# Attention and two feed-forward layers on one core: the places of three kinds of DMA in SyncE's queue, and the pools of three kinds of buffers

## The chip, the cores and the metric

The kernel runs on one core of one Trainium2 chip. The metric is the device time of one execution in microseconds; the median of several runs is taken. Lower is better.

## The reference, cut to what matters

```python
# 4 batches, 12 heads, 448 tokens, 64 per head; all float32
q_n, k_n = rmsnorm(q, g_q), rmsnorm(k, g_k)
scores = 1 / sqrt(64) * q_n @ k_n.T                 # per batch and head
attn = exp(scores - max(scores))
attn = attn / (sum(attn) + 1e-09)
x = (attn @ v)                                      # gathered to 1792 tokens x 768
h = x @ w_in;  x = (h * sigmoid(h)) @ w_out         # layer 1: 768 -> 2048 -> 768
h = x @ w_in2; out = relu(h) ** 2 @ w_out2          # layer 2: 768 -> 2048 -> 768
```

## The kernel before, in words

**Stages.** Attention comes first, over 24 pairs of heads (4 batches of 6 pairs). Layer 1 follows in eight segments, then layer 2 in two halves. Products of float32 are made of three products each: every operand is split into an upper and a lower part (`x_hi`/`x_lo`, `w_hi`/`w_lo`, helpers at L515, L517, L524).

**One pair in attention.** `prepare` loads queries and keys into one `qk` buffer (`load_qk`, L538; four such buffers), squares them on ScalarE (L549), sums (L558), takes the inverse root by Newton steps on GpSimd (L588 to L603), multiplies (`norm`, L612) and turns the result with TensorE (L624). `values` loads the values (`load_v`, L656). `weigh` makes the scores of 112 queries at a time (L677), their maxima (L688), the exponentials and their sums (L695), and turns the exponentials (L704). `attend` works on the sums: it inverts them on VectorE (L724, L725), stores them to DRAM (`store_r`, L732, buffer `rd`), and reads them back spread over 64 partitions for each of the two heads (`spread`, two DMAs at L741, buffer `R`, two of them). Meanwhile TensorE makes the products with the values in two blocks of 16 matmuls (L753), ScalarE copies them to `xf` (L503), and GpSimd multiplies by `R` (`attended`, L776). For the first two batches (12 pairs) the result is split at once into the operands of layer 1 (`x_hi` on ScalarE, L515; `x_lo` on GpSimd, L524). For the other 12 pairs it is stored to DRAM (`keep_x`, L808) and loaded again in layer 1 (`load_x`, L821).

**The order of the work.** A planner (class `Plan`) simulates the engines and writes out one order for each. Every step of attention has a nominal time: `PERIOD` (10.424) times the number of the pair, plus an entry of `LOADS` or `TABLE`, plus an entry of `FIRST` for the first four pairs. On each engine these fixed steps go out in the order of nominal times; the times themselves are not waited for. Steps without a nominal time (all weights, layer 1, layer 2) are put where the simulation finds them ready, and in front of a fixed step only if they end before that could begin. The simulation holds a DMA to land at its own time, plus `extra` for `store_r`. All DMAs are issued by SyncE, in one queue, and an instruction that waits there holds up all behind it.

**Weights.** A unit of weights is loaded in raw form into one of two `raw` buffers (`load_raw`, L869), made into words by one ScalarE instruction (L876) and four of VectorE (L880 to L896), written to DRAM (L904), and split (L515/L517, L524). The first two units are loaded at the start; the third needs the first `raw` buffer back, which its last reader (L896) frees.

**Pools.** Buffers made by `sa` lie in the pool `ap` of the attention stage, those by `sb` in `cp`, which lasts the whole run, or, if asked, in `yp`. `yp` takes the place of `ap`: the step `swap_pools` waits for every step that touches a buffer of `ap`, and each first use of a buffer of `yp` waits for that step. The hidden activations of layer 1 (`gg`), `part`, `V`, `xl` and `yf` are in `yp`. In layer 1, `up` multiplies into one of three PSUM banks `t` (L977); ScalarE takes the tanh (L989) and VectorE the product (L994) into one of four buffers `g` (in `cp`), and the split of `g` goes into `gg`. The second product of layer 1 is L1031; layer 2 has its products at L1193 and L1269.

Of the kernel before, what the change touches and what calls it, by code (L numbers as in the profile page):

```python
# [8 lines left out]
F32 = mybir.dt.float32  # L9
# [6 lines left out]
P = 128  # L16
CP = 112
# [4 lines left out]
NQ = 4  # L22

BEFORE = list(range(40, 72))
RINGS = {"xb": 4, "yb": 2, "yf": 6, "xl": 2, "v": 1, "V": 2, "part": 2, "xf": 6, "raw": 2, "W": 3, "w": 5, "E": 4, "PT": 4, "qk": 4, "T": 2, "n": 3, "vv": 3, "g": 4}

FORMS = ["raw", "word"]
CT = 2
# [9 lines left out]
FIT = 0.1  # L38
QUIET = 24.0
LOADS = {  # L40
    "load_g": [-27.0], "gains": [-3.0], "load_qk": [-38.0, -37.5], "load_v": [-10.0],
    "store_r": [12.5], "spread": [20.0, 20.4], "keep_x": [35.0],
}
TABLE = {
    "squares": [-25.39, -24.85],
# [48 lines left out]
class Step:  # L94
    def __init__(self, kind, on, fn, when, n):
        self.kind, self.on, self.fn, self.when, self.n = kind, on, fn, when, n
        self.needs, self.claims = {}, []
        self.at = min(on, key=lambda e: on[e][0])
        self.extra = 4.5 if kind == "store_r" else 0.0
        self.nom = None  # L100


# [278 lines left out]
def kernel(  # L381
# [18 lines left out]
    NCH = S // CP  # L400
# [27 lines left out]
    def sa(shape, dt, tag, n=None):  # L428
        return sb(shape, dt, tag, n, "ap")
# [234 lines left out]
    def weigh(i, T):  # L664

        PT = [sa([CP, NB8, CT, CP], F32, "PT") for _ in range(NCH // CT)]
        sums = sa([CP, 2, NCH], F32, "sum", 3)
        for c in range(NCH):
            at = ("pair", i, c)
            E = sa([CP, 2, S], F32, "E")  # L670
            pts = [psum("s"), psum("s")]

            def scores(e, c=c, pts=pts):
                for k_, (a, b_) in enumerate(((0, 0), (0, 1), (1, 0))):
                    for j in range(2):
                        r = slice(j * D, (j + 1) * D)
                        nc.tensor.matmul(  # L677
                            pts[j].ap[:CP, :S], T.ap[r, 0, a, c * CP:(c + 1) * CP], T.ap[r, 1, b_],
                            start=(k_ == 0), stop=(k_ == 2),
                        )  # L680

            step("scores", at, pe_t(0.606), scores, reads=[(T, (n, a)) for n in range(2) for a in range(2)], writes=pts)
            plan.fix(i, "scores", c)
            for j, pt in enumerate(pts):
                mx = sa([CP, 1], F32, "mx", 6)
                step(
                    "row_max", at, {"dve": (0.535, None, False)},
                    lambda e, pt=pt, mx=mx: nc.vector.tensor_reduce(  # L688
                        mx.ap, pt.ap[:CP, :S], AX.X, ALU.max, negate=True),
                    reads=[pt], writes=[mx],  # L690
                )
                plan.fix(i, "row_max", c, j)
                step(
                    "exp", at, {"act": (0.62, None, False)},
                    lambda e, j=j, c=c, pt=pt, mx=mx, E=E: nc.scalar.activation(  # L695
                        E.ap[:, j], pt.ap[:CP, :S], AF.Exp, bias=mx.ap, accum_out=sums.ap[:, j, c:c + 1]),
                    reads=[pt, mx], writes=[(E, j), (sums, (j, c))],
                )
                plan.fix(i, "exp", c, j)
                pe = psum("t")  # L700

                def turn(e, j=j, pe=pe, E=E):
                    for m in range(NCH):
                        nc.tensor.transpose(  # L704
                            pe.ap[:CP, m * CP:(m + 1) * CP], E.ap[:, j, m * CP:(m + 1) * CP], ident.ap)

                step("turn_e", at, pe_t(0.384), turn, reads=[(E, j), ident], writes=[pe])
                plan.fix(i, "turn_e", c, j)
                copy_step(
                    "e_copy", at, ECOPY[c][j], lambda c=c, j=j: PT[c // CT].ap[:, j * NCH:(j + 1) * NCH, c % CT, :],  # L710
                    lambda pe=pe: pe.ap[:CP, :S].rearrange("p (m t) -> p m t", t=CP), S, [pe], [(PT[c // CT], (c % CT, j))],
                )
                plan.fix(i, "e_copy", c, j)
        return PT, sums

    def attend(i, vr, PT, sums):
        b, hp = pairs[i]
        at = ("pair", i, NCH)
        keys = [(sums, (j, c)) for j in range(2) for c in range(NCH)]


        def inverse(e):
            r = sums.ap
            nc.vector.tensor_scalar(r, r, 1e-9, None, ALU.add)  # L724
            nc.vector.reciprocal(r, r)  # L725

        step("inverse", at, {"dve": (0.32, None, True)}, inverse, writes=keys)
        plan.fix(i, "inverse")
        rd = dram([2, NCH, CP], "rd", 3)
        step(  # L730
            "store_r", at, {"sp": (0.35, 0.8, False), "act": (0.35, 0.8, False)},
            lambda e: engine(e).dma_start(  # L732
                rd.ap.rearrange("j c p -> p (j c)"), sums.ap.rearrange("p j c -> p (j c)")),
            reads=keys, writes=[rd],
        )
        plan.fix(i, "store_r", at="sp")
        R = sa([P, S], F32, "R", 2)
        for j in range(2):
            step(
                "spread", at, small_dma,  # L740
                lambda e, j=j: engine(e).dma_start(  # L741
                    R.ap[j * D:(j + 1) * D, :],
                    rd.ap[j].rearrange("c p -> (c p)").unsqueeze(0).to_broadcast([D, S])),
                reads=[rd], writes=[(R, j)],
            )
            plan.fix(i, "spread", j=j, at="sp")
        pv = psum("pv")
        for c2, pt in enumerate(PT):

            def products(e, c2=c2, pt=pt):  # L750
                for m in range(NCH):
                    for j in range(2):
                        nc.tensor.matmul(  # L753
                            pv.ap[j * D:(j + 1) * D, c2 * CT * CP:(c2 + 1) * CT * CP],
                            vr.ap[:, j * NCH + m, :],
                            pt.ap[:, j * NCH + m].rearrange("p c t -> p (c t)"),
                            start=(m == 0),
                            stop=(m == NCH - 1),
                            skip_group_check=True,
                        )  # L760

            step(
                "attend", at, pe_t(1.456), products,
                reads=[vr] + [(pt, (c, j)) for c in range(CT) for j in range(2)], writes=[(pv, c2)],
            )
            plan.fix(i, "attend", c2)
        t = xf[b, hp] = sa([P, S], F32, "xf")


        copy_step(  # L770
            "pv_copy", at, ("act", "dve"), lambda: t.ap, lambda: pv.ap[:, :S], S,
            [(pv, c2) for c2 in range(len(PT))], [t])
        plan.fix(i, "pv_copy", at="act")
        step(
            "attended", at, any_t(S),
            lambda e: engine(e).tensor_tensor(t.ap, t.ap, R.ap, ALU.mult),  # L776
            reads=[(R, 0), (R, 1)], writes=[t],
        )
        plan.fix(i, "attended", at="pool")
# [32 lines left out]
    def make_x(b):  # L812
        x = [block(), block()]
        for hp in range(NP):
            t = xf[b, hp]
            at = ("pair", b * NP + hp, NCH)
            d, c = divmod(hp, HC)
            if b >= 2:
                k = xk[b, hp]
                t = sb([P, S], F32, "xl", None, "yp")  # L820
                step("load_x", at, dma_t(230), lambda e, k=k, t=t: engine(e).dma_start(t.ap, k.ap), reads=[k], writes=[t])  # L821
            split(
                ("x_hi", "x_lo"), at,
                lambda d=d, c=c: x[d].ap[:, 0, c, :], lambda d=d, c=c: x[d].ap[:, 1, c, :], lambda t=t: t.ap,
                [t], [(x[d], (0, c)), (x[d], (1, c))],
            )
            if b < 2:
                lower = plan.steps.pop()
                plan.fix(b * NP + hp, "x_hi", at="act")
                plan.steps.append(lower)  # L830
                plan.fix(b * NP + hp, "x_lo", at="pool")
        return x
# [244 lines left out]
    def combine(half, at, later):  # L1077
# [12 lines left out]
        def chunk(c, at, names):  # L1090

            f = {}
            for n in names:
                t = f[n] = sb([P, S], F32, "yf", None, "yp")
                d = yk[(ya, yb)[int(n[2]) - 1], (int(n[1]) - 1) * HC + c]
                step(
                    "load_y", at, dma_t(230), lambda e, t=t, d=d: engine(e).dma_start(t.ap, d.ap),
                    reads=[d], writes=[t],
                )
# [265 lines left out]
```

## Time and profile before

| | us |
|---|---|
| median of 3 runs | 1215.53 (1211.54 to 1215.88) |
| the profiled execution's own time | 1214.78 |
| its span, first to last instruction | 1212.7 |
| PE busy in the span | 1174.8 (97%) |
| DVE, ACT, POOL busy | 924.5, 542.5, 242.2 |
| mean granted TensorE clock | 0.996 of full speed |
| attention's first products with values, layer 1's first products | 29.10, 283.67 from the span's start |

PE is TensorE's matmuls, DVE VectorE, ACT ScalarE, POOL GpSimd, SP SyncE. The profile is one execution. The busy share of PE is a mean over stages and counts modelled ends, so that slowed matmuls count as busy; what a stage loses is better read from the starts of like instructions. A wait is put down to the event that came last.

### The profile page before, as it was taken

The numbers are of one execution on the slowest core, as the hardware profiler recorded it, in microseconds if no ns is written. First come the engines' busy times: TensorE is split into PE (matmuls) and PEld (weight loads), VectorE is DVE, ScalarE is ACT, GpSimd is POOL, SyncE is SP. The second block draws the span as 40 slices with busy tenths as digits, with TensorE's granted clock in tenths as the row PEclk, the third lists the DMA queues.
The fourth block names the chain that finished last, engine by engine and source line by source line (L and its number), as shares of the span: only waits on it lengthen the run. The fifth ranks groups of instructions, "written<-read, shape, count | busy, mean of one in ns | idle before, by whom it ended". The sixth has DMA issues, their size and how long they took to land.

```text
span 1212.7 us, 19013 instructions
## 1 busy us (share of the span) xinstructions
PE 1174.8 (97%) x6960; PEld 1049.1 (87%) x6960; DVE 924.5 (76%) x1614; ACT 542.5 (45%) x1138; POOL 242.2 (20%) x444
## 2 busy tenths in 40 slices
PE   4999999996999999999999999999999999999998
PEld 3777677665899999999999999899999999999998
DVE  7999899884989986979888959766667973555554
ACT  5999898782443332434333315343333534111111
POOL 3566676530000000112010001111111220000000
PEclk9999999999999999999999999999999999999999
DMA  6475676645675745696877747946556795434444
GB/s 152 81 87 86 77 83 106 91 70 100 211 219 169 218 138 169 206 356 210 256 245 245 246 140 250 397 141 250 197 195 229 258 322 200 162 143 143 144 155 131
DMA packets 134109, 220.75 MB, mean 182 GB/s; under 512 B 31104, under 2 KB 99456, under 8 KB 134016
## 3 DMA queue, kind: packets, MB, share of 16 engines
q1 hardware_dynamic: 134016, 219.54, 62.2%
q8 instruction: 55, 0.90, 0.4%
q14 instruction: 38, 0.31, 0.1%
HBM read 145.88 MB, written 73.62 MB: 181 GB/s over the span
## 4 chain that ended last, share of the span: by engine, by line
PE 86%; DMA 7%; DVE 3%; ACT 2%; SPq 1%; issue 1%; POOL 0%; ACTq 0%; POOLq 0%
PE s L1269 19%; PE s L1031 19%; PE t L977 19%; PE t L1193 12%; PE pv L1193 5%; PE t L704 4%; PE pv L753 4%; PE s L677 3%; DMA qk<-in_k_dram 3%; ACT E L695 1%; PE t L624 1%; DMA qk<-in_q_dram 1%; DMA raw<-in_moe_w_in_dram 1%; DMA rd<-sum 1%; DVE mx L688 1%
## 5 line engine op out<-in xcount | busy, mean ns | idle before, releaser
L977 PE MATMUL t<-xb,w 128*128 128x448 f32 x1152 | 240.9, 367 | 12.2 <-DVE g L994 12.2
L977 PEld LDWEIGHTS t<-xb,w 128*128 128x128 f32 x1152 | 217.2, 189 | 30.8 <-DVE g L994 13.3
L1031 PE MATMUL s<-gg,w 128*128 128x448 f32 x1152 | 239.7, 366 | 0.1
L1031 PEld LDWEIGHTS s<-gg,w 128*128 128x128 f32 x1152 | 216.1, 188 | 18.1 <-issue 0.4
L1269 PE MATMUL s<-w,gh 128*128 128x384 f32 x896 | 227.5, 334 | 0.0
L1269 PEld LDWEIGHTS s<-w,gh 128*128 128x128 f32 x896 | 162.3, 188 | 1.1
L1296 DVE TENSOR_TENSOR gg<-s,gg 128x384 f32<-128x384 f32 x196 | 107.6, 554 | 61.5 <-PE s L1269 61.1
L1269 PE MATMUL s<-w,gl 128*128 128x384 f32 x448 | 149.7, 334 | 0.0
L695 ACT ACTIVATE E<-s,mx 112x448 f32<-112x448 f32 x192 | 121.9, 646 | 22.2 <-ACT xf L503 14.9
L1209 DVE TENSOR_TENSOR g<-t,g 128x448 f32<-128x448 f32 x96 | 58.4, 620 | 80.6 <-ACT g L503 56.7
L688 DVE TENSOR_REDUCE mx<-s 112x1 f32<-112x448 f32 x192 | 107.3, 609 | 4.7 <-PE s L677 4.7
L704 PEld LDWEIGHTS t<-ident,E 112*112 112x112 f32 x768 | 73.5, 134 | 37.7 <-issue 16.9
L704 PE MATMUL t<-ident,E 112*112 112x112 f32 x768 | 96.7, 266 | 4.3 <-ACT PT L503 3.1
L524 DVE TENSOR_TENSOR w<-W,w 128x768 fp32r<-128x768 f32 (+1 forms) x99 | 86.3, 878 | 3.3 <-ACT w L515 2.2
L1269 PEld LDWEIGHTS s<-w,gl 128*128 128x128 f32 x448 | 84.1, 188 | 0.0
L753 PE MATMUL pv<-PT,vv 112*64 112x224 f32 x768 | 83.5, 359 | 0.0
L677 PE MATMUL s<-T 64*112 64x448 f32 x576 | 75.7, 387 | 4.5 <-ACT T L633 2.5
L524 POOL TENSOR_TENSOR w<-W,w 128x512 fp32r<-128x512 f32 (+1 forms) x13 | 19.4, 1495 | 283.2 <-ACT w L515 211.7
L515 ACT CAST w<-W 128x768 fp32r<-128x768 f32 (+1 forms) x57 | 42.7, 752 | 70.8 <-PE s L1031 41.1
L1219 ACT ACTIVATE g<-g 128x448 f32<-128x448 f32 x48 | 27.5, 575 | 97.0 <-DVE g L1209 96.4
L753 PEld LDWEIGHTS pv<-PT,vv 112*64 112x64 f32 x768 | 51.0, 136 | 20.3 <-DVE PT L505 0.3
L524 POOL TENSOR_TENSOR gl<-g,gh 128x448 fp32r<-128x448 f32 x12 | 14.7, 1224 | 266.6 <-DVE gh L517 199.1
(113 smaller groups left out, 1773.5 us busy)
## 6 DMA issues: line engine op xcount, KB each, us to landing
raw<-in_moe_w_in_dram SPq DMA_DIRECT2D x32, 768.0 KB, 5.3
raw<-in_moe_w_out_dram SPq DMA_DIRECT2D x24, 512.0 KB, 4.0
raw<-in_moe_w_out_dram SPq DMA_DIRECT2D x16, 768.0 KB, 5.0
su<-w SPq DMA_DIRECT2D x16, 768.0 KB, 7.6
w<-su SPq DMA_DIRECT2D x16, 768.0 KB, 4.2
yf<-y SPq DMA_DIRECT2D x48, 224.0 KB, 3.6
ki<-W SPq DMA_DIRECT2D x16, 384.0 KB
ko<-W SPq DMA_DIRECT2D x24, 256.0 KB
```

The source lines that it names most:

```text
L524: kind, when, any_t(n, rate), lambda e: engine(e).tensor_tensor(o(), a(), h(), ALU.subtract),
L677: nc.tensor.matmul(pts[j].ap[:CP, :S], T.ap[r, 0, a, c * CP:(c + 1) * CP], T.ap[r, 1, b_], start=(k_ == 0), stop=(k_ == 2),)
L688: lambda e, pt=pt, mx=mx: nc.vector.tensor_reduce(mx.ap, pt.ap[:CP, :S], AX.X, ALU.max, negate=True),
L695: lambda e, j=j, c=c, pt=pt, mx=mx, E=E: nc.scalar.activation(E.ap[:, j], pt.ap[:CP, :S], AF.Exp, bias=mx.ap, accum_out=sums.ap[:, j, c:c ...
L704: nc.tensor.transpose(pe.ap[:CP, m * CP:(m + 1) * CP], E.ap[:, j, m * CP:(m + 1) * CP], ident.ap)
L753: nc.tensor.matmul(pv.ap[j * D:(j + 1) * D, c2 * CT * CP:(c2 + 1) * CT * CP], vr.ap[:, j * NCH + m, :], pt.ap[:, j * NCH + m].rearrange("p ...
L977: nc.tensor.matmul(pt.ap[:, :S], w_()[:, c, :], x[c // HC].ap[:, a, c % HC, :], start=(c == 0 and n == 0), stop=(c == NC6 - 1 and n == 2),)
L1031: nc.tensor.matmul(pt.ap[:, :S], w_()[:, f, :], gg.ap[:, k, a, f, :], start=(f == 0 and n == 0), stop=(f == HQ - 1 and n == 2),)
L1193: nc.tensor.matmul(pt.ap[:, :S], w_()[:, c0 + c, :], view(b, a, c)(), start=(start and c == 0 and k == 0), stop=(c == HC - 1 and k == 2), ...
L1209: lambda e: nc.vector.tensor_tensor(o.ap, pt.ap[:, :S], a.ap, ALU.add),
L1269: nc.tensor.matmul(pt.ap[:, :NH], g.ap[:, fi, tc_ * P:(tc_ + 1) * P], w_()[:, 0, nh * NH:(nh + 1) * NH], start=(n == 0), stop=(n == 5),)
L1296: lambda e, o=o, pt=pt: nc.vector.tensor_tensor(o(), pt.ap[:, :NH], o(), ALU.add),
```

## The change

Six edits. `load_qk` goes from -38.0/-37.5 to -46.9/-46.4 and `spread` from 20.0/20.4 to 23.0/23.4 in the table of nominal times. The planner's allowance for the landing of `store_r` goes from 4.5 to 7.0. `sums`, `R` and `xf` are made by `sb` instead of `sa`, so that they lie in `cp`, and `swap_pools` no longer waits for their steps. `load_x` uses buffers of the ring `R` instead of `xl`, and `load_y` of layer 2 those of `xf` instead of `yf`; the numbers of buffers (2 and 6) stay.

```diff
-RINGS = {"xb": 4, "yb": 2, "yf": 6, "xl": 2, "v": 1, ... "xf": 6, ...}
+RINGS = {"xb": 4, "yb": 2, "v": 1, ... "xf": 6, ...}
...
 LOADS = {
-    "load_g": [-27.0], "gains": [-3.0], "load_qk": [-38.0, -37.5], "load_v": [-10.0],
-    "store_r": [12.5], "spread": [20.0, 20.4], "keep_x": [35.0],
+    "load_g": [-27.0], "gains": [-3.0], "load_qk": [-46.9, -46.4], "load_v": [-10.0],
+    "store_r": [12.5], "spread": [23.0, 23.4], "keep_x": [35.0],
 }
...
-        self.extra = 4.5 if kind == "store_r" else 0.0
+        self.extra = 7.0 if kind == "store_r" else 0.0
...
-        sums = sa([CP, 2, NCH], F32, "sum", 3)
+        sums = sb([CP, 2, NCH], F32, "sum", 3)
...
-        R = sa([P, S], F32, "R", 2)
+        R = sb([P, S], F32, "R", 2)
...
-        t = xf[b, hp] = sa([P, S], F32, "xf")
+        t = xf[b, hp] = sb([P, S], F32, "xf")
...
                 k = xk[b, hp]
-                t = sb([P, S], F32, "xl", None, "yp")
+                t = sb([P, S], F32, "R", 2)
                 step("load_x", at, dma_t(230), ...)
...
             for n in names:
-                t = f[n] = sb([P, S], F32, "yf", None, "yp")
+                t = f[n] = sb([P, S], F32, "xf")
```

## Rows read from the trace of the kernel before

**Rows 1.** PE's waits: us in total, times, longest us.
```profile
PE t L977 <- DVE g L994: 12.2, 1, 12.2
...
PE t L1193 <- DVE g L1209: 0.7, 1, 0.7
```
**Rows 2.** Busy us of each engine in a stretch; clock, DMA share, GB/s.
```profile
330.00:1212.70 882.70, 877.41 (x4498) 824.29 (x4496) 643.34 (x1079) 294.40 (x501) 83.17 (x59) 1.00 0.63 212
```
**Rows 3.** The chain of waits, in order of time: start us, us, what.
```profile
34.38 1.66 PE pv L753 x16
...
113.66 1.66 PE pv L753 x16
...
266.46 1.66 PE pv L753 x16
```
**Rows 4.** ACT's waits from 115 to 284 us.
```profile
ACT sq L549 <- DMA qk<-in_q_dram: 8.6, 6, 2.3
```
**Rows 5.** Timeline of SP's queue: start us, us, line, operation.
```profile
28.49 0.32 SPq L732 DMA_DIRECT2D rd<-sum  x1
...
106.24 0.40 SPq L732 DMA_DIRECT2D rd<-sum  x1
...
115.24 1.65 SPq L741 DMA_DIRECT2D R<-rd  x2
...
117.62 0.40 SPq L732 DMA_DIRECT2D rd<-sum  x1
...
289.33 0.48 SPq L732 DMA_DIRECT2D rd<-sum  x1
```
**Rows 6.** The waits of SP's queue, whole span.
```profile
SPq L741 <- DMA rd<-sum: 166.7, 23, 8.9
```
**Rows 7.** DMA issues by line: count, KB each, median us to landing.
```profile
raw<-in_moe_w_in_dram SPq DMA_DIRECT2D x32, 768.0 KB, 5.3
...
qk<-in_q_dram SPq DMA_DIRECT2D x24, 224.0 KB, 9.4
qk<-in_k_dram SPq DMA_DIRECT2D x24, 224.0 KB, 10.3
...
R<-rd SPq DMA_DIRECT2D x48, 112.0 KB, 3.9
```
**Rows 8.** The tile qk: landing of its loads.
```profile
DMA to landing us min/median/max: 8.2/9.4/11.2
```
**Rows 9.** Timeline of DVE, POOL and ACT around one pair.
```profile
113.03 0.20 DVE L725 RECIPROCAL sum<-sum 112x8 f32<-112x8 f32 x1
...
122.48 1.16 POOL L776 TENSOR_TENSOR xf<-xf,R 128x448 f32<-128x448 f32 x1
...
126.27 0.59 ACT L515 CAST xb<-xf 128x448 fp32r<-128x448 f32 x1
```
**Rows 10.** Timeline of DVE, PE, SP and ACT at layer 1's start.
```profile
277.43 0.94 DVE L896 SCALAR_TENSOR_TENSOR W<-raw,W 128x768 int32<-128x768 int32 x1
...
283.67 9.38 PE L977 MATMUL t<-xb,w 128*128 128x448 f32 x45
...
286.77 1.82 SPq L741 DMA_DIRECT2D R<-rd  x2
288.64 0.58 SPq L869 DMA_DIRECT2D raw<-in_moe_w_in_dram  x1
...
299.02 0.89 ACT L876 ACTIVATE W<-raw 128x768 f32<-128x768 f32 x1 [14.67 <-DMA raw<-in_moe_w_in_dram]
...
305.26 21.71 PE L977 MATMUL t<-xb,w 128*128 128x448 f32 x99 [12.20 <-DVE g L994]
```
**Rows 11.** Busy us of each engine in a stretch behind the stall.
```profile
305.00:308.00 3.00, 2.74 (x7) 2.48 (x8) 2.90 (x6) 0.65 (x2) 0.00 (x0) 0.50 0.95 329
```
**Rows 12.** The chain of waits at the start of the program.
```profile
6.32 0.46 SPq L656
...
7.33 5.71 DMA qk<-in_k_dram
```

More of the change, by code (lines that the diff above doesn't have):

```diff
@@ L24 @@
 BEFORE = list(range(40, 72))
-RINGS = {"xb": 4, "yb": 2, "yf": 6, "xl": 2, "v": 1, "V": 2, "part": 2, "xf": 6, "raw": 2, "W": 3, "w": 5, "E": 4, "PT": 4, "qk": 4, "T": 2, "n": 3, "vv": 3, "g": 4}
+RINGS = {"xb": 4, "yb": 2, "v": 1, "V": 2, "part": 2, "xf": 6, "raw": 2, "W": 3, "w": 5, "E": 4, "PT": 4, "qk": 4, "T": 2, "n": 3, "vv": 3, "g": 4}
 FORMS = ["raw", "word"]
```

## The prediction, made before the change was run

> **What bounds the kernel now.** I read the waits of TensorE first [rows 1]. After the first microseconds only one wait is long: 12.2 us before a matmul of L977, the start of layer 1; the longest in layer 2 is 0.7 us. From 330 us to the end PE is busy 877.41 of 882.70 us, so nothing can be won there beyond the end of the last stores [rows 2]. Two places are left, and the list of waits shows only one of them.
>
> The other is the attention stage, where I compare starts in the chain of waits [rows 3]. Each pair of heads has two blocks of 16 matmuls at L753. From 34.38 to 113.66 us there are 15 half pairs: 79.28 / 15 = 5.285 us each, 10.57 a pair. From 113.66 to 266.46 us there are 27, and 152.80 - 27 x 5.285 = 10.1 us more than that pace. The loss is spread over several short gaps and slowed matmuls, so a list of PE's waits hides it. The list of ScalarE's waits in that stretch names the cause: the squares of a pair wait for the load of its queries, 8.6 us in six times [rows 4]. Loads come too late.
>
> Why late? On SyncE's queue a pair's store of inverse sums is issued at 106.24, the loads of a later pair stand right behind it, and then the two spreads of the same sums stand at the head until 115.24, 9.0 us later; the next store is out only at 117.62 [rows 5], though its sums were ready at 113.03 + 0.20 = 113.23 us [rows 9]. The reader sees a queue that sleeps on a round trip through memory: 166.7 us in 23 times, for the landing of `rd` [rows 6]. The first of the 24 stores goes out at 28.49 and the last at 289.33 us, so SP's lap is 260.84 / 23 = 11.34 us against PE's 10.57. SP falls back 0.77 us a pair until the lead of the loads is used up, and then PE waits.
>
> **The change part by part.** *The order of SP's queue.* One pair is 10.424 us in the table. The spread goes from +20.0 to +23.0, the next pair's store stands at 12.5 + 10.424 = +22.9: the spreads now stand right behind the store of the next pair, one lap after their own. The wait they carry is then for something issued about 10.5 us before, where the wait shown ended 9.0 us after the store [rows 5]. So SP hardly sleeps; behind the spreads queue the store of x (last twelve pairs), the loads of queries and keys, the load of values and the next store, and all of them come at the time when their data are ready. The loads go from -38.0 to -46.9, 8.9 us earlier: from 12.6 to 21.5 us before the squares at -25.39. Landing takes 8.2 to 11.2 us [rows 8], so 1.4 us of slack (in the worst case) becomes 10.3. With four `qk` buffers an earlier load meets a new wait, the key norm of the pair four before; by the table that norm stands at -7.85, which is 2.6 us into a lap, and the load at 5.2, so I cost it at nothing. Gain: the 10.1 us, with bounds 0 and 10.1, since PE is never faster than 5.285 us a half. I take all of it because the cause is the late queue and not the transfers.
>
> *What the spread collides with.* R must be there when POOL scales the pair's output at 122.48 us, 9.25 us after the sums of the next pair (113.23). So far spreads land in 3.9 us; but queries and keys, which so far followed the store, land 9.4 and 10.3 us after issue (medians), more than twice that [rows 7]. The spreads take that place. Issued some 1.0 us behind the store, they land 10.4 to 11.3 us after it, so POOL waits 1.2 to 2.1 us. The cover is there: ScalarE casts that output (L515) at 126.27, and POOL would have ended at 122.48 + 1.16 = 123.64, 2.6 us of slack [rows 9]. At the slowest landing shown, 11.2 us [rows 8], POOL is 3.0 us late, 0.4 beyond the cover. Bounds: 0, and 12 pairs with such a cast x 0.4 = 4.8 us. I take 0.6, near the lower end, as both medians lie inside the cover. The Trainium skill speaks against the place chosen: its page "DMA: Bandwidth & Descriptors", section "Queues, rings and completion order", says that each DMA engine consumes the descriptors of a ring in order, so that nothing put behind the store on its engines starts before it. By that rule the spreads land no sooner than the store, as the loads do in this trace; by the 3.9 us of the spreads so far there would be no wait at all, and the sum would be 0.6 us lower.
>
> *The step into layer 1.* PE stops at 293.05 and goes on at 305.26, released by a DVE instruction (L994) [rows 1, 10]. Follow it back: DVE and ACT stand in their queues on the third raw weight block, which lands at 299.02, and from there to PE are 6.2 us. That load was issued at 288.64, behind the spread of pair 22, which waited for its sums until 286.77. Yet its buffer was free when L896 ended, 277.43 + 0.94 = 278.4 us. In the new order the spread of pair 22 stands behind the store of pair 23, and the planner takes the landing of a store to be 2.5 us longer (`extra` 4.5 to 7.0); so the free step, the load, fits in front of both. On the old clock it is issued at 278.4 instead of 288.64. With the median landing of 5.3 us [rows 7] PE could go on at 278.4 + 5.3 + 6.2 = 289.9, before 293.05: no stall. With the 10.4 us of this load it is 295.0, a stall of 2.0. I take 1.0 of the 12.2 to stay. With the stall goes the slow clock after it: granted 0.50 of full speed, the lower level, until 308 us [rows 11]: the 99 matmuls after the stall took 21.71 us, and at the 9.38 / 45 us of those before it they take 20.64, so 1.1 us. Together 12.2 + 1.1 = 13.3 off, 1.0 back.
>
> *Buffers of the whole run.* Sums, R and xf leave the pool that must end before layer 1's hidden buffers begin, so these wait for the last attention product and no longer for the last store of x. PE found no other wait there, so I cost it at nothing; what hides it are the three PSUM banks and four `g` buffers in between. The loads of x and y use R and xf again, as many buffers as before: nothing.
>
> *The start.* The keys of the fourth pair were issued at 7.33 and landed 5.71 us later [rows 12], and ACT worked on in its order only then. The values' load at 6.32 now comes behind them: one issue, 0.5 us, and 224 KB less in front. The landing moves by 0.5 to about 1.5 us; I take 1.0. Nothing as the lower bound, if another load is then the last.
>
> *All else.* The planner orders the remaining 885 us anew. The rows allow a gain of under 1 us [rows 1]; a loss is bounded by the one wait of this sort that the trace has, 12.2 us. I take 1.0, near the lower end, for a program whose other waits there are 0.7 us at most.
>
> **The sum**, against the profiled execution's own 1214.78 us (span 1212.7 and 2.1 around it; the median of the runs, 1215.53, is 0.06% higher, no difference here): 1214.8 - 10.1 + 0.6 - 13.3 + 1.0 - 1.0 + 1.0 = 1193.0 us.
>
> **The rivals.** *Attention keeps its loss.* If it is the transfers that need 11.3 us a lap, and not SP's sleep, loads are late in any order: 1193 + 10 = 1203. For it: the landing of 9 to 10 us of everything behind a store. Against: 2.4 us of each lap lie between the spread and the next store (115.24 to 117.62), a pure consequence of the sleep [rows 5].
>
> *The step into layer 1 stays.* If the planner leaves the raw load behind the spread of pair 22 after all, it goes out somewhere between 278.4 and 288.64; from the middle, 283.5, with the slow landing of 10.4, PE goes on at 300.1: 7.0 of stall, 1193 + 6 = 1199. If the order helps nothing, 1193 + 12 = 1205.
>
> *Neither works*: the two together, about 1215, no change.
>
> *Slower: the spreads behind the store.* One mechanism, at POOL's L776: R later than the 2.6 us cover delays ACT's cast, the exponentials stand behind it on ACT, and PE waits for these. Twelve pairs have the cast. To undo the 24.4 us of gains less 2.0 of other allowances takes 22.4 / 12 = 1.9 us a pair, R 9.25 + 2.6 + 1.9 = 13.75 us after the sums, a landing of 12.7 us; at 13.2 us the time is 1214.8 - 22.4 + 12 x 2.4 = 1221. The slowest load behind a store took 11.2. The ring rule of the Trainium skill (same page and section) leads here too, if the rings fill up.
>
> **How the numbers follow.** Forecast 0.62, its own range 1188 (all residues nothing, the start at 1.5) to 1199 (R at the slowest landing, or some waits in the new order). Attention keeps its loss 0.14, 1199 to 1206; the step stays, in part or whole, 0.15, 1197 to 1206; neither works 0.04; slower 0.05. The range of 8 in 10 is 1188 to 1205. Half a per cent is about what a measurement of this kernel can tell from no change: 1209.5 to 1221.6. Faster 0.91, same 0.04, slower 0.05.
>
> **What would show it.** Right: SP's wait for `rd` falls from 166.7 to below 50 us; stores one PE lap apart; no wait of ACT's squares for a load; half pairs of 5.285 us up to the end; layer 1's first wait under 3 us and no slow clock; POOL waiting 1 to 2 us for R in most pairs. Wrong: laps over 10.6 us, L515 waiting for POOL, PE waiting for L633 or L695, or a new wait of PE after 330 us.

## The result

| | before | after |
|---|---|---|
| median, us (same chip) | 1215.7 (1211.54 to 1218.09, 4 runs) | 1198.21 (1194.88 to 1200.38, 4 runs) |
| the profiled execution's own time | 1214.78 | 1194.88 |
| its span | 1212.7 | 1193.0 |

The ratio is 0.9857, with a 95% interval of 0.9821 to 0.9894. The forecast was 1193.0 us with a range of 1188 to 1205. The median gained 17.5 us; between the two profiled executions the gain is 19.9, and 21.8 had been forecast for these.

The two lists of waits come first. PE's long wait before layer 1 [rows 1] has shrunk to 3.5 us:

```profile
PE t L977 <- DVE g L994: 3.5, 1, 3.5
PE t L1193 <- ACT w L515: 1.0, 1, 1.0
```

SP's queue, whole span, its three waits in attention (columns as in the list before):

```profile
SPq L656 <- PE pv L753: 85.2, 19, 5.5
SPq L732 <- DVE sum L725: 76.1, 24, 9.7
SPq L741 <- DMA rd<-sum: 3.6, 1, 3.6
```

The wait for `rd` was 166.7 us in 23 times [rows 6] and is now 3.6 in one. SP still stands idle, 164.9 us by these three rows, but what ends its waits are TensorE's products (L753) and the sums (L725). It waits for data that are not there yet, and the store behind it isn't ready either: each of the 24 waits in its turn for its own sums.

The chain of waits (start us, us, what), with the same three blocks of 16 matmuls as in [rows 3]:

```profile
33.73 1.67 PE pv L753 x16
...
112.98 1.66 PE pv L753 x16
...
256.13 1.66 PE pv L753 x16
```

The first 15 half pairs take 79.25 / 15 = 5.283 us each, as before. The next 27 take 143.15, or 0.5 us more than that pace, where the kernel before lost 10.1.

The timeline of SP's queue (start us, us, line, operation), a lap in the middle and the step into layer 1:

```profile
28.28 0.32 SPq L732 DMA_DIRECT2D rd<-sum  x1
...
101.97 0.31 SPq L732 DMA_DIRECT2D rd<-sum  x1
102.38 1.16 SPq L741 DMA_DIRECT2D R<-rd  x2
...
112.64 0.31 SPq L732 DMA_DIRECT2D rd<-sum  x1
...
268.06 0.40 SPq L869 DMA_DIRECT2D raw<-in_moe_w_in_dram  x1
...
270.23 0.32 SPq L732 DMA_DIRECT2D rd<-sum  x1
270.64 1.49 SPq L741 DMA_DIRECT2D R<-rd  x2
...
272.88 0.39 SPq L869 DMA_DIRECT2D raw<-in_moe_w_in_dram  x1
...
277.56 0.38 SPq L869 DMA_DIRECT2D raw<-in_moe_w_out_dram  x1
```

The spreads now stand 0.4 us behind the next pair's store, with no sleep between. The lap is (270.23 - 28.28) / 23 = 10.52 us, where it was 11.34. The last store goes out 19.1 us earlier than in [rows 5], and the third raw weight block at 268.06, in front of the last store and of the spreads behind it; before, it went out at 288.64, behind such spreads [rows 10].

The timeline of PE at the start of layer 1 (in brackets: idle time before, and what ended it):

```profile
272.83 17.00 PE L977 MATMUL t<-xb,w 128*128 128x448 f32 x81
293.34 13.04 PE L977 MATMUL t<-xb,w 128*128 128x448 f32 x63 [3.50 <-DVE g L994]
```

And ACT in the same stretch, the first work on each raw block:

```profile
273.41 0.91 ACT L876 ACTIVATE W<-raw 128x768 f32<-128x768 f32 x1
...
284.69 0.91 ACT L876 ACTIVATE W<-raw 128x768 f32<-128x768 f32 x1 [4.20 <-DMA raw<-in_moe_w_in_dram]
...
289.03 0.66 ACT L876 ACTIVATE W<-raw 128x512 f32<-128x512 f32 x1 [1.66 <-DMA raw<-in_moe_w_out_dram]
```

The third block, issued at 268.06, is at work 5.35 us later without a wait. The fourth and fifth, issued at 272.88 and 277.56, are late: ACT waits for them until 11.8 and 11.5 us after the issue. The fifth lands 4.3 us after the fourth (289.03 - 284.69), so most of its lateness is the fourth's. They are what is late next, and they leave the 3.5 us.

The slow clock behind the stall is gone in this execution: the granted clock is 1.00 from 284 to 330 us, and the 63 matmuls behind the wait take 13.04 us. It comes back in the five profiles of the experiments below that have one such wait (order alone, spread alone, old allowance, last two stores from ACT, after once more): there the same 63 take 14.59 to 14.60 us behind waits of 2.3 to 3.8. PE's timeline in after, once more:

```profile
294.78 14.60 PE L977 MATMUL t<-xb,w 128*128 128x448 f32 x63 [3.55 <-DVE g L994]
```

The granted clock there is 0.94 from 273 to 300 us. So this part of the gain, 1.1 us by the forecast, is the luck of one execution.

The gain adds up. Layer 1 starts 283.67 - 272.83 = 10.84 us earlier. Its first 144 products end at 293.34 + 13.04 = 306.38, where they ended at 305.26 + 21.71 = 326.97 [rows 10]: 20.59 earlier, so 9.75 were won behind its start. To the end of the span 19.7 are left, so the rest of the program gives 0.9 back.

### The profile page after: what moved, and what is told of

It reads as the page before. It is cut to its first block, busy times and chain, and to the rows that moved or that the text cites. A ratio compares the mean times of both kernels' runs of the same rounds, so it can differ in the third digit from the quotient of the medians.

```text
span 1193.0 us, 19008 instructions
## 1 busy us (share of the span) xinstructions
PE 1169.5 (98%) x6960; PEld 1047.8 (88%) x6960; DVE 921.9 (77%) x1610; ACT 543.3 (46%) x1140; POOL 245.1 (21%) x446
## 4 chain that ended last, share of the span: by engine, by line
PE 94%; DVE 3%; DMA 2%; ACT 1%; SPq 0%; issue 0%; ACTq 0%
PE s L1269 20%; PE s L1031 18%; PE t L977 18%; PE t L1193 12%; PE t L704 7%; PE pv L753 6%; PE s L677 6%; PE pv L1193 5%; PE t L624 2%; DMA raw<-in_moe_w_out_dram 1%; DMA W<-kp 0%; DMA qk<-in_k_dram 0%; DVE W L896 0%; SPq L538 0%; DVE gg L524 0%
## 5 line engine op out<-in xcount | busy, mean ns | idle before, releaser
L977 PE MATMUL t<-xb,w 128*128 128x448 f32 x1152 | 240.3, 366 | 3.5 <-DVE g L994 3.5
L1031 PE MATMUL s<-gg,w 128*128 128x448 f32 x1152 | 240.2, 366 | 0.1
L977 PEld LDWEIGHTS t<-xb,w 128*128 128x128 f32 x1152 | 216.0, 188 | 22.8 <-DVE g L994 4.6
L1031 PEld LDWEIGHTS s<-gg,w 128*128 128x128 f32 x1152 | 216.1, 188 | 18.7 <-issue 0.4
L753 PE MATMUL pv<-PT,vv 112*64 112x224 f32 x768 | 83.0, 359 | 0.0
L515 ACT CAST w<-W 128x768 fp32r<-128x768 f32 (+1 forms) x61 | 45.1, 743 | 75.7 <-PE s L1031 48.9
L524 POOL TENSOR_TENSOR w<-W,w 128x512 fp32r<-128x512 f32 (+1 forms) x13 | 19.1, 1468 | 279.0 <-ACT w L515 219.5
L753 PEld LDWEIGHTS pv<-PT,vv 112*64 112x64 f32 x768 | 51.1, 136 | 19.7
```

The lines of the kernel that those rows point to most:

```text
L524: kind, when, any_t(n, rate), lambda e: engine(e).tensor_tensor(o(), a(), h(), ALU.subtract),
L753: nc.tensor.matmul(pv.ap[j * D:(j + 1) * D, c2 * CT * CP:(c2 + 1) * CT * CP], vr.ap[:, j * NCH + m, :], pt.ap[:, j * NCH + m].rearrange("p ...
L977: nc.tensor.matmul(pt.ap[:, :S], w_()[:, c, :], x[c // HC].ap[:, a, c % HC, :], start=(c == 0 and n == 0), stop=(c == NC6 - 1 and n == 2),)
L1031: nc.tensor.matmul(pt.ap[:, :S], w_()[:, f, :], gg.ap[:, k, a, f, :], start=(f == 0 and n == 0), stop=(f == HQ - 1 and n == 2),)
```

## The experiments

My theory: SP's sleep on the landing of `rd` is the cause of both losses, the place of the spread ends it, and the pools, the allowance and the place of R's landing bring or cost next to nothing. Rivals: the earlier loads alone are enough; the pools let layer 1 start earlier; the transfers set the pace of attention. Later ones concern the 3.5 us that stay. The first four kernels below after ran on one chip, the next four on a second, the last four on a third; the ratio is to the kernel before on the same chip.

| kernel | median us | ratio [95%] | attention, us | wait at L977, us |
|---|---|---|---|---|
| before | 1215.7 | | 254.6 | 12.2 |
| after | 1198.21 | 0.9857 [0.9821, 0.9894] | 244.4 | 3.5 |
| order alone | 1199.33 | 0.9827 [0.9777, 0.9878] | 244.5 | 3.8 |
| pools alone | 1223.44 | 1.0018 [0.9989, 1.0047] | 258.5 | 13.5 |
| spread alone | 1200.85 | 0.9837 [0.9775, 0.9898] | 245.8 | 3.4 |
| loads alone | 1218.36 | 0.9979 [0.9951, 1.0008] | 253.0 | 17.5 |
| old allowance | 1194.7 | 0.9777 [0.9731, 0.9823] | 244.4 | 2.3 |
| spread before the store | 1200.45 | 0.9822 [0.9782, 0.9862] | 245.2 | 4.3 |
| last two stores from ACT | 1201.77 | 0.9829 [0.9784, 0.9874] | 244.4 | 3.6 |
| all stores from ACT | 1206.78 | 0.9884 [0.9835, 0.9934] | 251.2 | 7.1 |
| last store turned | 1192.96 | 0.9785 [0.9748, 0.9821] | 244.4 | 0 |
| all stores turned | 1195.58 | 0.9792 [0.9746, 0.9838] | 246.0 | 0 |
| last turned, old allowance | 1194.33 | 0.9803 [0.9767, 0.9839] | 244.4 | 1.3 |
| after, once more | 1199.13 | 0.9829 [0.9793, 0.9864] | 245.2 | 3.6 |

"Attention" is the time from the first products with values (L753) to the first of layer 1 (L977) in PE's timeline. It and the wait come from one profile each. Rows of different chips should not be ranked by differences of a few us: the lowest ratio, 0.9777, belongs to a kernel that still has the wait.

**The order alone** (before, with the places and the allowance of after, and the old pools):

```diff
-    ... "load_qk": [-38.0, -37.5], ...
-    ... "spread": [20.0, 20.4], ...
+    ... "load_qk": [-46.9, -46.4], ...
+    ... "spread": [23.0, 23.4], ...
-        self.extra = 4.5 if kind == "store_r" else 0.0
+        self.extra = 7.0 if kind == "store_r" else 0.0
```

> Order and allowance as after the change, pools as before. Theory (order alone): as after the change, 1195 to 1200 us, the wait at L977 3 to 5 us. Rival (the pool's end): if the first hidden buffers waited for the last store of x, the wait at L977 stays over 8 us and the time is 1203 or more.

It has the whole gain: the ratio, the length of attention and the wait at L977 are those of after within what the runs tell apart.

**The pools alone** (before, with `sums`, `R`, `xf` made by `sb`, and `load_x` and `load_y` in their rings):

```diff
-        sums = sa([CP, 2, NCH], F32, "sum", 3)
+        sums = sb([CP, 2, NCH], F32, "sum", 3)
...
-                t = sb([P, S], F32, "xl", None, "yp")
+                t = sb([P, S], F32, "R", 2)
```

> Pools as after the change, order and allowance as before. Theory (order alone): no gain, 1212 to 1218 us; SP waits some 160 us for rd, half pairs lose about 10 us, the wait at L977 is 10 to 13 us. Rival (the pool's end): the wait at L977 falls to 4 us or less and the time to about 1205.

No gain against the kernel before on that chip, 1222.42 us, which lay above the expected range itself. SP sleeps as before. Its list of waits, whole span:

```profile
SPq L741 <- DMA rd<-sum: 172.5, 23, 8.7
```

**The spread alone** (before, with the place of the spread and the allowance):

```diff
-    ... "spread": [20.0, 20.4], ...
+    ... "spread": [23.0, 23.4], ...
-        self.extra = 4.5 if kind == "store_r" else 0.0
+        self.extra = 7.0 if kind == "store_r" else 0.0
```

> Only the spread and the allowance are moved; loads of queries and keys and the pools as before. Theory (SP's sleep): SP laps at PE's pace, and a lead of 12.6 us covers a landing of 8 to 11; attention loses 0 to 2 us, 1196 to 1201. Rival (the lead of the loads): attention still loses 8 us or more, 1204 to 1208.

This is nearly the whole gain. SP's list of waits in this kernel:

```profile
SPq L732 <- DVE sum L725: 81.2, 24, 14.6
SPq L656 <- PE pv L753: 81.0, 18, 5.6
...
SPq L741 <- DMA rd<-sum: 3.8, 1, 3.8
```

The sleep is gone without touching the loads, and SP's lap, from the first store to the last, is 10.61 us. Attention is 1.3 us longer than in after, of which its list of waits shows one wait of ACT's squares (L549) for keys, 1.0 us. By these two profiles the earlier loads are worth about 1 us once the spread has moved, below what the medians tell apart.

**The loads alone** (before, with the loads moved and nothing else):

```diff
-    ... "load_qk": [-38.0, -37.5], ...
+    ... "load_qk": [-46.9, -46.4], ...
```

> Only the loads of queries and keys are moved; spread, allowance and pools as before. Theory (SP's sleep): SP still laps in 11.3 us, the longer lead is eaten up more slowly, attention loses 0 to 4 us near its end, and the 12 us wait at L977 stays: 1204 to 1209. Rival (the lead of the loads is all): attention loses nothing and the wait at L977 goes too, 1195 to 1200. Rival (the transfers set the lap): 1213 or more.

This was a miss of my theory: I had taken the late loads to be what costs attention its 10 us, so that loads issued 8.9 us earlier would bring much of it back. They brought 1.7 by the two profiles, and even that may be scatter: before and the pools alone, with the same order, differ by 3.9. PE's waits in this kernel, and POOL's wait for R from 30 to 295 us, in two fences:

```profile
PE t L977 <- DVE g L994: 17.5, 1, 17.5
...
PE t L624 <- POOL n L612: 2.7, 3, 1.9
...
PE pv L753 <- DMA vv<-in_v_dram: 0.9, 1, 0.9
```

```profile
POOL xf L776 <- DMA R<-rd: 56.9, 14, 10.0
```

No square waits for a load any more; [rows 4] are gone. In their place POOL waits 14 times for R, PE for POOL's norm (L612) and for values. SP still sleeps 172.7 us in 23 times, so its lap is still too long, 11.45 us, and whatever it issues late is late next: now the spreads and the values. The wait for `qk` in the kernel before was the first sign of the late queue, not the cause. The stall before layer 1 even grew, from 12.2 to 17.5 us.

**The old allowance** (after, with `extra` back at 4.5). The prediction held the longer allowance to be why the raw block fits in front of the last store.

```diff
-        self.extra = 7.0 if kind == "store_r" else 0.0
+        self.extra = 4.5 if kind == "store_r" else 0.0
```

> As after the change, with the allowance for the store back at 4.5. The prediction's step (the allowance lets the raw load go in front): the raw load falls behind the spread, the wait at L977 grows to 6 us or more, 1201 to 1206. Rival (the place of the spread alone does it): the load stays in front, as after the change, 1195 to 1200.

The raw blocks, the last store and the last spreads go out in the same order, and the wait at L977 is 2.3 us. The allowance isn't needed; the place of the spread does it alone.

**The spread before the store** (after, with the spreads just in front of the next pair's store instead of behind it). This separates R's landing from the store that goes ahead of it.

```diff
-    ... "spread": [23.0, 23.4], ...
+    ... "spread": [22.8, 22.9], ...
```

> As after the change, with the spread just in front of the next pair's store instead of just behind it. Theory (what is behind a store lands with it): the spreads land in 3 to 5 us instead of 7 to 8, POOL waits less, and the time is the same within 2 us, 1195 to 1200, since POOL's waits were covered. Rival (R's landing cost time): 3 us or more faster than after the change, under 1194.

No difference that can be measured. SP now waits for `rd` again, in short pieces:

```profile
SPq L741 <- DMA rd<-sum: 24.2, 14, 5.0
```

They cost nothing that shows: up to the last two stores the lap is 10.66 us, near PE's pace, and attention is 245.2 us. So the place before the store gains nothing either: the landing behind it is covered.

**The last two stores from ACT** (after, the stores of the last two pairs issued from ACT's queue). Why do raw blocks four and five land so late? If they stand behind the last store in SP's queue, another queue for the store frees them. If the store holds the DMA engines or the memory itself, it doesn't matter who issues it.

```diff
-        plan.fix(i, "store_r", at="sp")
+        plan.fix(i, "store_r", at="act" if i >= 22 else "sp")
```

> As after the change, but the stores of the sums of the last two pairs are issued by ACT instead of SP. Theory (raw loads are slow because they stand behind a store in SP's rings): raw loads at layer 1's start land in 4 to 7 us, the wait at L977 falls from 3.5 to under 1 us, 1192 to 1196. Rival (the engines or the memory are held by the store, on any queue): the raw loads land as late as after the change, the wait stays 2 to 5 us, 1196 to 1200.

The wait stays. The timeline of ACT:

```profile
269.45 0.32 ACTq L732 DMA_DIRECT2D rd<-sum  x1
...
285.03 0.91 ACT L876 ACTIVATE W<-raw 128x768 f32<-128x768 f32 x1 [4.94 <-DMA raw<-in_moe_w_in_dram]
...
288.25 0.68 ACT L876 ACTIVATE W<-raw 128x512 f32<-128x512 f32 x1 [0.55 <-DMA raw<-in_moe_w_out_dram]
```

SP issues these two blocks at 272.09 and 277.17, so ACT has them 12.9 and 11.1 us later, as late as with the store in SP's own queue (11.8 and 11.5). Standing behind it in one queue is not the reason. The Trainium skill bears on this: by its page "DMA: Bandwidth & Descriptors", section "Issuing engines are not separate DMA queues", DMAs from different engines run on the same 16 DMA engines in the end. These landings, late from either queue, agree.

**All stores from ACT:**

```diff
-        plan.fix(i, "store_r", at="sp")
+        plan.fix(i, "store_r", at="act")
```

> As after the change, but all 24 stores of the sums are issued by ACT. Theory (rings): loads of queries and keys and the spreads land in 3 to 6 us instead of 7 to 10; ACT issues 24 times some 0.35 us in a stage in which it is over 90% busy, which costs 0 to 8 us: 1192 to 1206. Rival (the engines are held on any queue): landings stay at 7 to 10 us.

Worse than after. Attention is 6.8 us longer, with no single wait of PE over 1.1 us in it; the profile is of the slowest of the four runs, 1213.92 us. The stores stand in ACT's order of work and go out one lap of (275.82 - 27.6) / 23 = 10.79 us apart, and SP waits for `rd` again, 21.1 us in 12 times. That the loss comes from this is argued, not shown. PE's wait at L977 grows to 7.1 us in two times. A separate queue for the store helps nowhere.

**The last store turned.** The 112 x 8 inverse sums are stored so that each of the 896 values is a piece of 4 bytes of its own in DRAM. Here the last pair's sums are turned by TensorE, copied by ACT, and stored as 8 rows of 448 bytes.

```diff
+TURNED = (23,)
...
+        if i in TURNED:
+            tr, sT = psum("t"), sa([NB8, CP], F32, "sT", 1)
...
+                lambda e: nc.tensor.transpose(tr.ap[:NB8, :CP], sums.ap.rearrange("p j c -> p (j c)"), ident.ap),
...
+            copy_step("r_copy", at, ("act",), lambda: sT.ap, lambda: tr.ap[:NB8, :CP], CP, [tr], [sT])
...
+                lambda e: engine(e).dma_start(rd.ap.rearrange("j c p -> (j c) p"), sT.ap),
...
+        else:
```

> As after the change, but the inverse sums of the last pair are turned on PE (one matmul of 112 columns), copied by ACT, and stored as 8 rows of 448 bytes instead of 896 pieces of 4 bytes; all else as after the change. Theory (the small pieces hold the DMA engines, on whichever queue): the raw loads behind it land in 4 to 7 us instead of 11 to 12, the wait at L977 falls from 3.5 to under 1 us, 2 to 4 us faster than after the change in this call. Rival (raw loads are slow by their own 768 KB and the other transfers there): they land in 9 us or more, the wait stays 2 to 5 us, and the time is that of after the change.

The wait is gone. In the following fences L997 is the old L977, L896 the old L876, L889 the old L869, and L745 the turned store. First PE's timeline, one unbroken run of all 144 products:

```profile
272.77 29.43 PE L997 MATMUL t<-xb,w 128*128 128x448 f32 x144
```

SP's queue in the same kernel:

```profile
272.79 0.39 SPq L889 DMA_DIRECT2D raw<-in_moe_w_in_dram  x1
...
273.86 0.34 SPq L745 DMA_DIRECT2D rd<-sT  x1
...
278.74 0.40 SPq L889 DMA_DIRECT2D raw<-in_moe_w_out_dram  x1
```

And ACT on these two blocks:

```profile
279.51 0.91 ACT L896 ACTIVATE W<-raw 128x768 f32<-128x768 f32 x1 [5.01 <-DMA raw<-in_moe_w_in_dram]
...
283.36 0.69 ACT L896 ACTIVATE W<-raw 128x512 f32<-128x512 f32 x1 [0.69 <-DMA raw<-in_moe_w_out_dram]
```

The fourth block, issued at the same time as in after, is there 6.7 us later instead of 11.8, the fifth 4.6 us instead of 11.5. The busy row of 276 to 280 us (the last three numbers are the clock, the busy share of the DMA engines and GB/s), first in after, then here:

```profile
276.00:280.00 4.00, 4.00 (x21) 3.62 (x21) 2.98 (x4) 0.05 (x1) 0.00 (x0) 1.00 1.11 55
```

```profile
276.00:280.00 4.00, 4.00 (x22) 3.70 (x21) 3.86 (x5) 0.49 (x1) 0.28 (x1) 1.00 0.78 254
```

By these rows the DMA engines of after are busy throughout and move 55 GB/s; here they move 254. With the last two stores from ACT it is 0.86 and 59 GB/s, so the engines are held in the same way from the other queue. By itself this doesn't separate the small pieces from the later store: turning takes time, so the store stands 1.1 us behind the fourth block and no longer in front of it.

**All stores turned** (`TURNED = tuple(range(24))`, else the same) puts the turned store in front of a raw block, and takes small pieces away in all of attention, so it also tests the rival that transfers set its pace.

> As the kernel with the last store turned, for all 24 pairs. Theory (small pieces hold the engines): nothing waits for R or for a load in attention, and the DMA share of the stage falls; but PE gets 24 more matmuls of about 0.1 us and one more user of the three banks t, ACT 24 more copies of about 0.2 us at over 90% busy: 0 to 8 us slower than with the last one alone. Rival (1 KB loads are slow by themselves): the DMA share stays.

SP's queue, with a raw block 0.4 us behind a turned store:

```profile
269.64 0.28 SPq L745 DMA_DIRECT2D rd<-sT  x1
270.02 0.40 SPq L889 DMA_DIRECT2D raw<-in_moe_w_in_dram  x1
```

ACT takes it up without a wait:

```profile
275.34 0.90 ACT L896 ACTIVATE W<-raw 128x768 f32<-128x768 f32 x1
```

It landed within 5.3 us, right behind a store. In after, block four had the store of 4-byte pieces, the spreads and the store of x ahead of it and took 11.8 us. With only spreads and store of x ahead a block took 6.7 us (last store turned) and 7.1 (last turned, old allowance), with only a turned store ahead 5.3 at most. Block four of this kernel has all three ahead of it, with the store turned and 4.4 us ahead instead of 2.6, and ACT takes it up without a wait too, so it landed within 7.8 us (its issue by SP, then ACT):

```profile
274.05 0.39 SPq L889 DMA_DIRECT2D raw<-in_moe_w_in_dram  x1
```

```profile
281.87 0.90 ACT L896 ACTIVATE W<-raw 128x768 f32<-128x768 f32 x1
```

What is left to hold it up is the store in its old form. The second question is read from the busy time in 30 to 115 us (clock, DMA share and GB/s at the end), first in after, then here:

```profile
30.00:115.00 85.00, 85.00 (x774) 63.85 (x773) 79.69 (x154) 79.86 (x211) 55.05 (x133) 1.00 0.52 87
```

```profile
30.00:115.00 85.00, 85.00 (x778) 63.39 (x776) 77.84 (x152) 80.42 (x217) 54.83 (x133) 1.00 0.30 87
```

The DMA share falls from 0.52 to 0.30 at the same 87 GB/s, and attention is no faster (246.0 against 244.4 and 245.2 us). Transfers don't set its pace; that rival had fallen with the spread alone, which makes the same transfers. The difference prices a store in its old form against a turned one: 0.22 of 16 engines over a lap of 10.5 us, an estimate of 37 engine microseconds for 896 pieces, 3.6 KB. Spread evenly that would be 2.3 us on each engine, less than the 5 us that block four lost; how the pieces lie on the engines is not shown.

**The last store turned, with the old allowance**, beside **after once more** on the same chip:

```diff
+TURNED = (23,)
...
-        self.extra = 7.0 if kind == "store_r" else 0.0
+        self.extra = 4.5 if kind == "store_r" else 0.0
```

> The last store turned, and the allowance for stores back at 4.5. If the allowance has no effect, as after the change showed with 4.5, this is within 2 us of the kernel with the last store turned; if 4.5 itself gives a better order in layers 1 and 2, it is 3 us or more faster.

> The changed kernel once more, to have it on this chip beside the others: 1195 to 1200 us, a wait at L977 of 2 to 5 us.

In time the two allowances can't be told apart here either. In the order they can: with 4.5 the third raw block falls behind the spread of pair 22 and goes out at 270.78 us instead of 267.97, and a wait of 1.3 us at L997 comes back. After, once more, has its wait again, 3.6 us. On this chip the last store turned is the fastest, 1192.96 us (1190.22 to 1197.26) against 1199.13 (1195.61 to 1201.28) for after: 6.2 us between the medians, where 2 to 4 had been expected. Between their two profiled executions (spans 1188.3 and 1195.8) 1.7 of the 7.5 us are the start of layer 1, and 5.5 its first 144 products, which end 294.78 + 14.60 - 274.44 = 34.94 us after their start in after and 29.43 with the store turned: 3.6 of wait and the slow clock behind it. These 5.5 belong to the edit by what was shown. The intervals of the two ratios overlap a little, so a gain over after of about 5 us is likely and not settled.

## Why the prediction was right, and where it was off

**SP's sleep and the lap.** Right. The wait for `rd` fell to 3.6 us, below the 50 that were named, stores are one PE lap apart, and attention gained 254.6 - 244.4 = 10.2 us against 10.1. The spread alone gives nearly all of it, the loads alone 1.7 us at most. Off was the weight of the two edits: the prediction let the gain rest in part on the loads' slack of 10.3 us, while their move is worth about 1 us once the spread has moved.

**What the spread collides with.** 0.6 us was put down for POOL's wait for R; nothing was lost to it. From 30 to 275 us POOL waits for R 16.9 us in three times, but 16.7 of these are the last two, where it has no other work left; the sign that was named, 1 to 2 us in most pairs, didn't come. PE has no wait from it, and the spread before the store gains nothing. The landing did get longer, as forecast, but by less: where POOL's wait shows it, R is there 7.3 to 9.0 us after the first spread's issue (251.10 to 258.37, 260.94 to 268.58, 81.11 to 90.08), against 3.9 before and the 9.4 to 10.3 that were taken. The rule of the Trainium skill that the prediction weighed (page "DMA: Bandwidth & Descriptors", section "Queues, rings and completion order": nothing behind the store on its engines starts before it) agrees with these landings and made no difference to the time: with the spread in front of the store or behind it, it is the same.

**The step into layer 1.** The mechanism was right. The third raw block goes out in front of the last store, 0.02 us after its buffer is free (L896 ends at 267.09 + 0.95 = 268.04). The term that was mis-sized is the residue: 1.0 us was taken and a first wait under 3 us named as a sign, and it was 3.5. The prediction followed one load, the third block; what was late next were blocks four and five, issued behind the store of 4-byte pieces. That the slow clock went too was luck: it is gone in the profiled execution of after and back, behind a wait of much the same length, in the repeat. And the reason given for the order, the planner's longer allowance, isn't needed: in after the old allowance gives the same order. The mechanism itself exists, for with the last store turned the allowance does decide whether the block goes in front of the spread.

**The buffers of the whole run.** Right: nothing, by the pools alone and by the order alone.

**The start.** 1.0 was taken, 0.65 measured (L753 first at 28.38 instead of 29.03 in PE's timeline). One profile doesn't settle it: after, once more, starts at 29.29. Over all profiles, the eleven with the loads moved start at 28.03 to 29.29, the three without at 29.03 to 29.89.

**All else.** 1.0 was taken, 0.9 measured. The longest wait there is 1.0 us of L1193 for ACT, where 0.7 stood before [rows 1], so most of the 0.9 has no wait to its name and lies inside the scatter of the last section. By that scatter, 8.8 us in layer 1's products without a wait, a busy PE from 330 us on doesn't show that nothing can be won there.

**The rivals.** That attention keeps its loss to transfers falls with the spread alone, and again with all stores turned. That the spreads behind the store slow the kernel falls with the spread before the store. The sum was 1.9 us too low on the profiled executions: the residue's 2.5 too little, less the 0.6 too much for R; the other terms came within 0.4 each. The median was another 3.3 us above the profiled execution, which is one run and was the fastest of the four. On the third chip the repeat of after is 20.3 us faster than the kernel before, between the 17.5 of the first measurement and the 21.8 forecast. The low end of the forecast's own range, 1188, doesn't follow from what is named for it: all residues nothing and the start at 1.5 give 1214.8 - 10.1 - 13.3 - 1.5 = 1189.9.

## What to carry to other kernels

When a queue sleeps on a round trip through memory, compare its lap with that of the engine that sets the pace: the sleep does harm only while it makes the lap the longer one, and moving one waiting instruction a lap back can end it. Moving the first transfer that is late (here the loads) only shows the next late one; move what the queue sleeps on. And when a stall goes, follow the two or three transfers behind the one that ended it, with the landing that they have at their new places. Read a short stretch, such as a slow clock behind a stall, in more than one execution.

## What the runs showed of the hardware

**A store of many small pieces holds other transfers up.** A raw block 2.6 us behind 3.6 KB in pieces of 4 bytes landed 11.8 us after its issue with the store in SP's queue and 12.9 with it in ACT's, and in 276 to 280 us the DMA engines moved 55 and 59 GB/s; 0.4 us behind a store of 8 rows of 448 bytes it was 5.3 us at most. The distance counts: the third block of after, 7.5 us behind such a store (260.53 to 268.06), was there within 5.35 us. In the kernel before, the third block took 10.4 us with such a store 0.7 us behind it [rows 5, 10]; whether one just behind holds a block up too, no run separates. The Trainium skill, page "DMA: Bandwidth & Descriptors", section "Specifications", names 512 bytes as the least size for full rate, with a read-modify-write below it; both kinds of piece lie below that, and no run here shows whether it is the reason.

**The kernel before scatters.** Its medians on the three chips of the experiments were 1222.42, 1219.71 and 1219.4 us, with 37 single runs from 1210.76 to 1228.05; after stayed within 1194.88 to 1201.28 in nine. The pools alone, with the old order, had an attention 3.9 us longer than the profile of before. That the scatter sits in the round trips is not shown: the loads alone, with the same sleep, stayed within 1213.77 to 1220.38 in ten runs, and all stores from ACT, with 21.1 us of it, ran from 1203.45 to 1213.92 in four.

**Layer 1's products take 479 to 488 us without a wait behind it.** The groups of L977 and L1031 (busy us, mean ns, idle before) in the last store turned:

```profile
L997 PE MATMUL t<-xb,w 128*128 128x448 f32 x1152 | 239.6, 366 | 0.0
L1051 PE MATMUL s<-gg,w 128*128 128x448 f32 x1152 | 239.1, 365 | 0.0
```

and in the same kernel with the old allowance:

```profile
L997 PE MATMUL t<-xb,w 128*128 128x448 f32 x1152 | 243.9, 368 | 1.3 <-DVE g L1014 1.3
L1051 PE MATMUL s<-gg,w 128*128 128x448 f32 x1152 | 243.6, 368 | 0.0
```

487.5 against 478.7 us, at a granted clock of 1.00, with as many products of the same shape; the spans differ by 9.9. Such a difference is larger than most of the small effects above, and its cause stays open.
